# Plain key blocks for near heads, outputs turned by TensorE and a new order in an attention and maxout-FFN kernel

## The chip, the core and the metric

The kernel runs on one core of one Trainium2 chip. The metric is device time in microseconds (us) of one execution; a kernel's time is the median of its runs. Engines are called as in the profile: PE (TensorE matmul), PEld (its weight loads), DVE (VectorE), ACT (ScalarE), POOL (GpSimd) and SP (SyncE, which here only issues DMAs).

## What is computed

Attention over 4 batches, 8 heads, 768 positions, 64 values a head; then a feed-forward layer. Three heads (`is_retrieval` is 1 for heads 0, 2, 6) see all earlier keys. The other five, the near heads, see the 4 first keys (`n_sink`) and the last 64 (`window`).

```python
causal = rel >= 0                      # rel = query - key
stream_keep = causal & (is_sink | in_win)
scores = np.where(mask, scale * q @ k.T, -1e9)
a = softmax(scores); attn = a @ v      # (4, 8, 768, 64)
x = attn.transpose(0, 2, 1, 3).reshape(4 * 768, 512)
h = np.maximum(np.maximum(x @ w1, x @ w2), x @ w3)   # w: 512 x 768
out = h @ w_out                        # 768 x 512, result 3072 x 512
```

## The kernel before

The kernel assumes which heads are near (`GUESS`), computes on that assumption in `fast`, and at the end reads a count of differences; only if it is not zero, `general` computes all anew. Everything of interest is in `fast`. No scheduler decides anything: the tuple `PROGRAM` (line 84) lists 486 steps, and each step emits its instructions at once. So each engine and each DMA queue executes its share strictly in the order of PROGRAM, and a step whose input is late holds up all that follows it on that engine.

Each batch is cut into two halves of 384 queries. Batch 0 goes another way than the others, since it must start from nothing. The steps (table at line 807):

- `hl half hp n`: load K and Q of `n` pairs of heads (line 198), on SP or ACT. For `n` = 2 the staging tiles come from a pool with two buffers each for K and Q, so the third such load waits until the casts of the first have been done.
- `cast half hp xy`: K and Q of a pair to f16 (line 216), K by the first engine named, Q by the second (d DVE, a ACT, p POOL). The tile is position-major, so the copy also exchanges the order of head and position.
- `turnp`: turn K and Q of a pair by TensorE into PSUM, and copy out by the engines named (line 228). `tr` tiles, V's `vb`, the AV results and the feed-forward results share four PSUM banks (`bank`, line 190).
- `s0 half u hp`: scores of batch 0, unit `u` of a pair (line 581). `FIRST_UNITS` lists its key blocks: kind `p` is a plain block of 128 keys, kind `c` a block put together of the sink keys and the 64 keys before a block's middle (`kx0` makes it, line 555). In half 0 the masks are added by TensorE, as a product of the identity with blocks of `far` (0 or -30000; `FIRST_FAR`); then ACT takes Exp into a `pt` tile. Score tiles have two PSUM buffers.
- `k0`: masks of batch 0's half 1, by multiplication (line 634).
- `load_v`: V (line 290). `vc` casts, `vt` sorts V's rows by TensorE (batch 0 alone), `v` casts for other batches, `y` fills `vx`, V's rows for the `c` blocks (line 512).
- `load b quad`: K and Q of batches 1 to 3 for four heads, on POOL's queue (line 248); `turn` transposes a part of them on DVE (line 264, 1.1 us each); `kx` makes their `c` blocks.
- `s`, `k`: scores with Exp and masks of batches 1 to 3 (lines 639 and 696).
- `av b half hp [D]`: probabilities times V, a reciprocal and a product on DVE (line 703); with `D`, a transposing DMA on SP's queue makes `xT`; without it, `x` turns the result by TensorE and a copy (line 736). Seven of the eight results of batch 0's half 1 and batch 1's half 0 go by DMA (from `av 0 1 0 D` to `av 1 0 3 D`), `av 0 1 3` and all of batch 0's half 0 by TensorE.
- `f b half wi ni`: one of 3 x 6 products of a half with a block of w1, w2 or w3 (line 434), with the maximum taken on DVE; `o`: the output product, a copy and the write (line 454).
- `w wi`: load a weight with a cast on POOL's queue. `gs`, `gp`: a tiny copy that holds SP's or POOL's queue until a weight or a load is there. `idle n`: matmuls of zeros. `check`, `verdict`, `read`, `flags`, `guess`: the test of the assumption.

## Time and profile before

| what | value |
|---|---|
| median of 3 runs (lowest, highest) | 195.14 us (192.91, 195.88) |
| the profiled execution | span 195.2 us |
| instructions | 4739 |
| PE busy | 180.9 us, 93% |
| DVE, ACT, POOL busy | 145.0, 98.8, 81.8 us |
| HBM read, written | 25.17 MB, 6.29 MB |

In the profile, a row of a timeline is: start in us, duration in us, engine, line, operation, out<-in, shape, count, and in brackets the idle time before it with what released it. A row of the chain is start, duration, engine, tile and line: the work that ended last, followed back. A row of a group has after the count the busy total in us, the mean of one in ns, and the idle time before it. A row of stretches has the stretch in us, its length, then the busy time and instruction count of PE, PEld, DVE, ACT and POOL, the granted clock of TensorE, the DMA share and GB/s. A row of DMA issues ends with the KB of one and the median us from issue to landing.

### The profile page before, as it was taken

What the parts mean: (1) busy time and instruction counts of PE and PEld (TensorE: products, weight loads), DVE (VectorE), ACT (ScalarE), POOL (GpSimd) and SP (SyncE); (2) the same over time, 40 slices, a digit from 0 to 9 for tenths busy, and PEclk for the clock granted to TensorE, in tenths of its full rate; (3) what the DMA queues carried; (4) which work ended last, traced back from release to release, by engine and by line L of the source; (5) the groups of instructions that cost most, each with busy time, mean ns of one, the idle gap of its engine ahead of it and who ended that gap; (6) DMA issues with size and microseconds to landing.
All of it is one profiled execution on the core that took longest, in us unless ns stands there. A gap on an engine that the chain in (4) does not pass through costs nothing.

```text
span 195.2 us, 4739 instructions
## 1 busy us (share of the span) xinstructions
PE 180.9 (93%) x1854; PEld 106.1 (54%) x1854; DVE 145.0 (74%) x308; ACT 98.8 (51%) x158; POOL 81.8 (42%) x140
## 2 busy tenths in 40 slices
...
GB/s 177 329 325 267 207 213 207 116 164 189 160 187 227 97 133 158 242 99 108 210 167 241 93 58 0 77 114 57 0 66 129 0 57 59 134 0 54 161 54 116
DMA packets 44248, 26.59 MB, mean 136 GB/s; under 512 B 31038, under 2 KB 39742, under 8 KB 44222
## 3 DMA queue, kind: packets, MB, share of 16 engines
...
HBM read 25.17 MB, written 6.29 MB: 161 GB/s over the span
## 4 chain that ended last, share of the span: by engine, by line
PE 66%; DMA 12%; DVE 11%; SPq 5%; issue 2%; ACT 1%; ACTq 0%; DVEq 0%
PE yy L437 34%; PE yy L462 15%; DMA vs<-in_v_dram 8%; PE oacc L717 6%; PE st L674 5%; DMA qs<-in_q_dram 4%; SPq L302 4%; DVE KQ L272 4%; PE yst L437 3%; DVE x L724 2%; DVE acc L449 1%; PE yst L462 1%; DVE KQ L241 1%; SPq L283 1%; DVE vx L800 1%
## 5 line engine op out<-in xcount | busy, mean ns | idle before, releaser
L377 POOL TENSOR_TENSOR pt<-pt,kb 128x512 f16<-128x512 f16 (+5 forms) x53 | 48.3, 931 | 67.4 <-ACT pt L691 55.5
L691 ACT ACTIVATE pt<-st 128x1024 f16<-128x1024 f32 (+2 forms) x51 | 43.5, 908 | 24.6 <-PE st L674 24.2
L437 PE MATMUL yy<-xT,w2t 128*128 128x384 f16 x184 | 36.8, 330 | 0.0
L437 PE MATMUL yy<-xT,w0t 128*128 128x384 f16 x180 | 34.9, 326 | 0.6 <-DMA xT<-x 0.6
L437 PE MATMUL yy<-xT,w1t 128*128 128x384 f16 x176 | 34.4, 326 | 0.1
L462 PE MATMUL yy<-woutt,hT 128*128 128x512 f16 (+1 forms) x138 | 32.8, 384 | 0.0
L449 DVE TENSOR_TENSOR hT<-yy,acc 128x384 f16<-128x384 f32 x46 | 25.2, 555 | 6.8 <-PE yy L437 5.1
L449 DVE TENSOR_TENSOR acc<-yy,acc 128x384 f16<-128x384 f32 x44 | 24.0, 555 | 7.9 <-PE yy L437 4.0
L272 DVE STREAM_TRANSPOSE KQ<-kq 128x384 f32<-128x384 f32 x24 | 25.4, 1134 | 0.4 <-DMA kq<-in_q_dram 0.4
L437 PEld LDWEIGHTS <-w0t 128*128 128x128 f16 x192 | 18.1, 98 | 13.5 <-issue 1.7
L445 ACT CAST acc<-yy 128x384 f16<-128x384 f32 x27 | 12.9, 489 | 23.3 <-PE yy L437 21.2
L437 PEld LDWEIGHTS <-w1t 128*128 128x128 f16 x192 | 17.9, 98 | 12.3 <-issue 1.0
L437 PEld LDWEIGHTS <-w2t 128*128 128x128 f16 x192 | 17.8, 98 | 12.3 <-issue 0.9
L462 PEld LDWEIGHTS <-hT 128*128 128x128 f16 x150 | 14.8, 101 | 16.5 <-issue 2.0
L717 PE MATMUL oacc<-va,pt 128*128 128x65 f16 x392 | 19.1, 195 | 4.4 <-ACT va L478 3.5
L717 PEld LDWEIGHTS <-pt 128*128 128x128 f16 x472 | 17.6, 98 | 8.3 <-issue 4.4
L471 ACT COPY ot<-yy 128x512 f32<-128x512 f32 (+1 forms) x14 | 7.9, 566 | 23.6 <-PE yy L462 20.9
L724 DVE TENSOR_TENSOR x<-oacc,sums 128x384 f16<-128x384 f32 x32 | 17.8, 557 | 1.1
L629 ACT ACTIVATE pt<-st 128x1024 f16<-128x1024 f32 (+5 forms) x22 | 15.5, 760 | 3.1 <-PE st L608 2.9
L674 PE MATMUL st<-KQ 32*128 32x128 f16 (+2 forms) x342 | 15.3, 263 | 0.0
L377 DVE TENSOR_TENSOR pt<-pt,kb 128x256 f16<-128x256 f16 (+4 forms) x31 | 11.7, 383 | 1.8 <-ACT pt L691 1.7
L445 DVE CAST acc<-yy 128x384 f16<-128x384 f32 x18 | 10.0, 557 | 3.8 <-PE yy L437 3.3
...
## 6 DMA issues: line engine op xcount, KB each, us to landing
...
kq<-in_q_dram POOLq DMA_DIRECT2D x3, 288.0 KB, 10.0
...
```

Of the source, the lines that this page charges most:

```text
L272: nc.vector.transpose(out=dst.rearrange("c (p j) -> c j p", j=n)[:, j0:j1], in_=src.rearrange("c (j i) -> c j i", i=R),)
L377: engine.tensor_tensor(out=x, in0=x, in1=of_blocks(kb, pattern, rows), op=ALU.mult)
L437: nc.tensor.matmul(yy[:, 0:HALF], w_t[wi][:, ks, ni * P : (ni + 1) * P], xT[b, half, ks].rearrange("p a t -> p (a t)"), start=(ks == 0), s ...
L445: op(out=acc[b, half, ni], in_=yy[:, 0:HALF])
L449: nc.vector.tensor_tensor(out=acc[b, half, ni] if wi == 1 else hT[b, half, ni], in0=yy[:, 0:HALF], in1=acc[b, half, ni], op=ALU.max,)
L462: nc.tensor.matmul(yo[:, 0:n], hT[b, half, ns][:, tb * P : (tb + 1) * P], woutt[:, ns, c : c + n], start=(ns == 0), stop=(ns == NNB - 1),)
L471: op(out=ot[:, c : c + n], in_=yo[:, 0:n])
L629: nc.scalar.activation(out=pts[0, half, hp, u][:, r0:r1, c0:c1], in_=sts[hp][:, r0:r1, c0:c1], func=AF.Exp, scale=sc,)
L674: nc.tensor.matmul(sts["XY"[g // 2]][:, g % 2, c0 : c0 + n * P], KQ[rows, 0, ki * P : (ki + 1) * P] if kind == "p" else kx[b % 2][quad][ro ...
L691: nc.scalar.activation(out=pts[b, s, xy][:, r0:r1, c0:c1], in_=st[:, r0:r1, c0:c1], func=AF.Exp, scale=sc,)
L717: nc.tensor.matmul(o[:, i, r, 0 : D + 1], at[b, h, kind, ki, qi], vv[:, 0 : D + 1], start=(n == 0), stop=(n == len(todo) - 1), skip_group_ ...
L724: nc.vector.tensor_tensor(out=x, in0=o[:, :, :, 0:D], in1=rc.unsqueeze(3).to_broadcast([P, HB, 2, D]), op=ALU.mult,)
```

## The change

It does five things. In batch 0's half 0 the near heads take plain key blocks (`FIRST_UNITS`, `av`), with the sinks and the window in the mask that TensorE adds; so `far` has six blocks, `kx0` and `y` serve batch 0 only from the third block on, and the retrieval and near heads of a pair get the same columns. Casts of K and Q write through the exchanged view and read the staged tile as it lies. All outputs of batch 0's half 1 and batch 1's half 0 are turned by TensorE. There is no `gs` step any more, `guess` is the last but one step. And PROGRAM is written in a new order throughout; of it the diff below shows the first part and the end.

```diff
@@ -59,7 +59,7 @@
 FIRST_UNITS = [
     {
         "R": [[("p", 0, 0, 3, 0), ("p", 2, 2, 1, 384)], [("p", 1, 1, 2, 0)]],
-        "S": [[("p", 0, 0, 2, 0), ("p", 1, 1, 1, 256), ("c", 1, 2, 1, 384)], [("p", 2, 2, 1, 0)]],
+        "S": [[("p", 0, 0, 3, 0), ("p", 2, 2, 1, 384)], [("p", 1, 1, 2, 0)]],
     },
     {
         "R": [
@@ -74,7 +74,7 @@
         ],
     },
 ]
-FIRST_FAR = {"R": [[(0, "C"), (384, "C")], [(0, "C")]], "S": [[(0, "B0 W B W")], [(0, "B")]]}
+FIRST_FAR = {"R": [[(0, 0, 1), (384, 0, 1)], [(0, 0, 1)]], "S": [[(0, 1, 4)], [(0, 4, 2)]]}
 FIRST_KEEP = {
     ("R", 0): (384, "C"), ("R", 1): (384, "C"), ("R", 3): (0, "C"),
     ("S", 0): (0, "W B W B"), ("S", 1): (0, "W B"),
@@ -82,71 +82,74 @@
 LEAST, MOST = 1.0e-9, 16.0
 
 PROGRAM = (
-    "idle 11, hl 0 2 2 sc, cast 0 1 pd, turnp 0 1 aa, cast 0 0 dd, cast 0 2 dp, load_v 0 0 0 4 s",
-    "load_v 0 0 4 4 s, turnp 0 0 ad, cast 0 3 pa, cleark 0 p, cleark 1 d, kx0 0 1 p, s0 0 1 1",
-    "s0 0 0 0, hl 1 0 2 ss, idle 1, turnp 0 3 da, turnp 0 2 da, s0 0 1 0, kx0 0 3 p, s0 0 0 3",
-    "vc 0 0 4 p, vc 0 4 4 p, s0 0 0 1, kx0 0 2 p, s0 0 0 2, hl 1 2 2 ss, cast 1 0 dd",
-    "turnp 1 0 dd, cast 1 3 dd, load 1 0, vt 0 02 da, cast 1 2 aa, vt 0 1 a, cast 1 1 pp",
-    "turnp 1 1 d, w 0, y 0 0 1:4:2 r p, s0 0 1 2, s0 0 1 3, y 0 0 4:5:1 r r, turnp 1 3 ad",
-    "s0 1 3 0, y 0 0 5:8:2 s r, clear 0 d, kx0 1 1 p, y 0 0 1:4:2 s p, s0 1 1 1, load_v 0 1 s",
-    "turnp 1 2 dd, kx0 1 2 r, av 0 0 1, s0 1 2 0, y 0 0 5:8:2 r r, kx0 1 3 r, w 1, gs 1, s0 1 0 1",
-    "av 0 0 0, av 0 0 3, s0 1 0 2, x 0 0 1 d, x 0 0 0 d, load 1 1, s0 1 3 2, vc 1 0 4 p",
-    "x 0 0 3 a, y 0 0 4:5:1 s p, av 0 0 2, vc 1 4 4 p, s0 1 0 0, s0 1 0 3, vt 1 1 a, turn 1 0 0 0",
-    "clear 1 p, k0 1 1 2 p, x 0 0 2 d, vt 1 02 ad, turn 1 0 1 1, turn 1 0 0 1, s0 1 1 0",
-    "k0 0 0 2 p, k0 0 1 2 d, f 0 0 0 3 a, k0 1 0 2 p, f 0 0 0 1 a, s0 1 1 3, w 2, y 0 1 1:4:2 r p",
-    "s0 1 1 2, y 0 1 4:5:1 r r, gs 0, k0 0 3 2 d, f 0 0 0 5 a, kx 1 0 a, k0 2 1 0 p, turn 1 0 1 0",
-    "k0 3 0 2 p, av 0 1 0 D, av 0 1 1 D, f 0 0 0 4 a, turn 1 1 0 0, turn 1 1 0 1, f 0 0 0 2 a",
-    "f 0 0 0 0 a, f 0 0 1 0, load 2 0, f 0 0 1 5, turn 1 1 1 1, s0 1 2 2, k0 2 0 1 p",
-    "turn 1 1 1 0, f 0 0 1 3, f 0 0 1 2, k0 2 0 0 p, y 0 1 5:8:2 r a, f 0 0 1 1, k0 3 1 2 p",
-    "f 0 0 1 4, s 1 0, av 0 1 2 D, kx 1 1 p, k0 2 1 1 p, k0 2 3 1 p, av 0 1 3, f 0 0 2 0",
-    "f 0 0 2 1, s 1 1, f 0 0 2 5, k 1 0 X 1 d, k 1 1 Y 0 p, f 0 0 2 2, turn 2 0 0 0, f 0 0 2 4",
-    "turn 2 0 1 0, x 0 1 3 a, s 1 2, f 0 0 2 3, f 0 1 0 5 a, f 0 1 0 3 a, k 1 1 X 1 p",
-    "turn 2 0 1 1, f 0 1 0 1 d, s 1 7, k 1 2 X 0 p, f 0 1 0 2 d, flags, load_v 1 0 s, v 1 0 0 d",
-    "y 1 0 1:8:2 s a, v 1 0 1 a, gs 0, k 1 2 Y 0 d, y 1 0 4:5:1 s r, k 1 0 Y 0 p, f 0 1 0 0 d",
-    "w 3, v 1 0 2 d, f 0 1 1 2, s 1 3, f 0 1 2 2, f 0 1 1 1, load_v 1 1 s, k 1 3 Y 0 p, f 0 1 1 3",
-    "f 0 1 2 3, y 1 0 4:5:1 r a, y 1 0 1:8:2 r a, gs 0, f 0 1 0 4 d, s 1 5, k 1 0 X 0 d",
...
-    "f 3 0 1 5, f 3 0 2 0, f 3 1 0 4 a, f 3 1 0 3 a, f 3 1 1 4, read, f 3 0 2 5, f 3 1 0 1 d",
-    "f 3 1 0 5 d, f 3 1 0 0 a, f 3 1 0 2 d, f 3 1 1 2, f 3 1 1 3, f 3 1 1 5, gs 0, o 2 1 0 a",
-    "f 3 1 1 0, f 3 1 2 0, o 3 0 1 d, o 3 0 2 d, o 3 0 0 a, f 3 1 2 2, f 3 1 2 3, f 3 1 1 1",
-    "f 3 1 2 1, f 3 1 2 4, f 3 1 2 5, o 3 1 0 a, o 3 1 1 a, o 3 1 2 d, idle 1",
+    "clear 0 p, cast 0 0 pp, idle 6, hl 0 2 2 sc, turnp 0 0 dd, s0 0 0 0, cast 0 1 pd, idle 1",
+    "load 1 0, turnp 0 1 da, s0 0 0 1, hl 1 0 2 ss, s0 0 1 0, cast 0 3 pp, turnp 0 3 da",
+    "s0 0 0 3, s0 0 1 3, cast 1 0 dp, turnp 1 0 dd, s0 0 1 1, s0 1 0 0, cast 0 2 dd",
+    "cast 1 1 pd, turn 1 0 1 1, turnp 1 1 d, k0 0 0 2 d, idle 1, s0 1 3 0, turn 1 0 0 0",
+    "turnp 0 2 ad, turn 1 0 0 1, cleark 0 d, s0 1 1 0, w 0, load 1 1, idle 1, hl 1 2 2 ss",
+    "cast 1 2 pa, s0 1 2 0, turnp 1 2 aa, kx0 2 d, s0 0 1 2, idle 1, load_v 0 0 4 4 s",
+    "vc 0 4 4 d, cast 1 3 ap, load_v 0 0 0 4 s, s0 0 0 2, s0 1 0 2, vc 0 0 4 d, turnp 1 3 dd",
+    "kx0 3 d, vt 0 02 dd, y 0 0 5:8:2 s d, kx0 1 a, vt 0 1 a, s0 1 0 1, av 0 0 1, s0 1 1 1",
+    "av 0 0 0, s0 1 1 3, k0 2 0 1 p, load_v 0 1 s, vc 1 4 4 a, av 0 0 2, idle 1, k0 0 1 2 p",
+    "vc 1 0 4 p, y 0 0 4:5:1 s p, w 1, x 0 0 0 a, k0 1 0 2 p, clear 1 d, av 0 0 3, vt 1 1 a",
+    "x 0 0 2 d, x 0 0 3 d, s0 1 1 2, k0 0 3 2 d, turn 1 0 1 0, x 0 0 1 a, vt 1 02 aa",
+    "y 0 1 5:8:2 r p, s0 1 3 2, y 0 0 1:4:2 s d, turn 1 1 0 0, s0 1 2 2, f 0 0 0 3 a",
+    "k0 2 3 1 p, turn 1 1 0 1, f 0 0 0 1 a, f 0 0 0 2 a, k0 2 0 0 d, turn 1 1 1 0",
+    "f 0 0 0 0 a, kx 1 0 p, f 0 0 0 4 a, turn 1 1 1 1, s0 1 0 3, k0 3 0 2 d, y 0 1 4:5:1 r r",
+    "gp 1 2, y 0 1 1:4:2 r p, k0 1 1 2 p, f 0 0 0 5 a, av 0 1 1, k0 3 1 2 p, s 1 0, av 0 1 0",
+    "k0 2 1 1 p, av 0 1 3, x 0 1 1 a, k0 2 1 0 p, av 0 1 2, x 0 1 0 a, cleark 1 p, s 1 1",
+    "load_v 1 0 s, y 1 0 1:8:2 s r, w 2, x 0 1 3 d, k 1 1 X 0 d, f 0 0 1 3, f 0 0 1 0",
+    "kx 1 1 p, k 1 0 X 1 p, k 1 0 Y 0 d, f 0 0 1 1, x 0 1 2 a, flags, s 1 2, f 0 1 0 1 d",
+    "f 0 1 1 1, k 1 2 X 1 d, f 0 0 1 5, f 0 0 1 2, s 1 4, f 0 1 2 1, load_v 1 1 s",
+    "f 0 1 0 3 a, y 1 1 4:5:1 r p, k 1 1 Y 0 d, k 1 1 X 1 d, y 1 0 1:8:2 r p, v 1 0 2 a",
+    "f 0 0 2 1, k 1 2 X 0 p, v 1 0 3 d, y 1 0 4:5:1 r r, v 1 0 0 r, y 1 1 1:8:2 r p",
+    "f 0 0 2 2, k 1 2 Y 0 d, s 1 3, f 0 0 1 4, v 1 1 3 p, f 0 0 2 4, load 2 0, f 0 0 2 5",
+    "k 1 0 X 0 d, f 0 0 2 0, k 1 4 X 1 p, f 0 1 1 3, f 0 1 2 3, w 3, av 1 0 0",
+    "y 1 0 4:5:1 s a, s 1 5, k 1 5 X 1 d, f 0 1 0 0 d, av 1 0 3, f 0 1 0 2 a, av 1 0 2",
+    "v 1 0 1 a, f 0 0 2 3, s 1 7, k 1 7 X 0 p, k 1 7 Y 1 p, av 1 0 1, f 0 1 0 4 d, load 2 1",
...
+    "f 2 1 2 2, f 3 0 1 5, f 3 0 2 5, f 2 1 2 1, check, f 3 0 0 4 a, o 2 1 2 d, o 2 1 0 a",
+    "f 3 1 0 3 d, f 3 0 1 4, f 3 1 2 4, verdict, f 3 1 1 3, o 2 1 1 d, f 3 1 0 0 a, f 3 1 2 3",
+    "read, f 3 0 2 4, o 3 0 0 a, o 3 0 2 d, f 3 1 0 2 a, f 3 1 1 2, f 3 1 1 0, f 3 1 2 0",
+    "f 3 1 0 1 a, f 3 1 1 1, f 3 1 2 1, f 3 1 2 2, o 3 0 1 a, f 3 1 2 5, o 3 1 1 d, o 3 1 0 d",
+    "o 3 1 2 a, idle 1, guess, idle 1",
 )

@@ -217,7 +220,7 @@
         cast[half, hp] = []
         for nm, src, op in zip(("kn", "qn"), staged.pop((half, hp)), engines):
             x = half16.tile([P, HB, 2, D], FP16, tag=nm, name=nm)
-            op(out=x, in_=src.rearrange("p h j d -> p j h d"))
+            op(out=x.rearrange("p j h d -> p h j d"), in_=src)
             cast[half, hp].append(x)
 
     def of_pair(hp):
@@ -327,6 +330,10 @@
     nc.vector.memset(warm, 0.0)
     nc.scalar.activation(out=warm, in_=warm, func=AF.Exp)
 
+    far = consts.tile([P, 6, P], FP16, name="far")
+    nc.vector.memset(far[:, 3], -FAR)
+    if n_sink > 0:
+        nc.vector.memset(far[0:n_sink, 3], 0.0)
     kb = consts.tile([P, len(BLOCKS), P], FP16, name="kb")
     nc.gpsimd.memset(kb, 1.0)
     nc.gpsimd.affine_select(
@@ -351,13 +358,18 @@
     )
     for x in (kb[:, 0:1], kb[:, 5:7]):
         nc.vector.tensor_copy(out=x, in_=kb[:, 3:4].to_broadcast([P, x.shape[1], P]))
+
+    def as_far(dst, src):
+        nc.vector.tensor_scalar(
+            out=dst, in0=src, scalar1=FAR, scalar2=-FAR, op0=ALU.mult, op1=ALU.add
+        )
+
+    as_far(far[:, 5], kb[:, 4])
     if n_sink > 0:
         nc.vector.tensor_copy(out=kb[0:n_sink, 0], in_=kb[0:n_sink, 2])
         nc.vector.memset(kb[0:n_sink, 1:5:3], 1.0)
-    far = consts.tile([P, 5, P], FP16, name="far")
-    nc.vector.tensor_scalar(
-        out=far, in0=kb[:, 0:5], scalar1=FAR, scalar2=-FAR, op0=ALU.mult, op1=ALU.add
-    )
+    as_far(far[:, 1:3], kb[:, 0:2])
+    as_far(far[:, 0:5:4], kb[:, 2:4])
 
     def pick(at0, rows, row, a, sa, b, sb):
         inner = [[1, b * P]] if sb == 1 else [[sb * P, b], [1, P]]
@@ -510,22 +522,24 @@
             op(out=va[0][:, :, half * HB + i, 0:D], in_=vb.rearrange("p (h d) -> p h d", d=D))
 
     def prep_x(b, half, heads, what, op):
-        by_row = b == 0 and half in sorted_halves
-        vs = staged_v[b, half] if not by_row else va[0][:, :, half * HB : (half + 1) * HB, 0:D]
+        first = 1 if b == 0 else 0
+        vs = staged_v[b, half] if b else va[0][:, :, :, 0:D]
         dst = vx[b % 2]
         hs = slice(*map(int, heads.split(":")))
         which = list(range(*hs.indices(H)))
         xs_ = slice(near.index(which[0]), near.index(which[-1]) + 1)
         n = len(which)
         assert near[xs_] == which
-        if what == "r":
+        if what == "r" and b == 0:
+            op(out=dst[64:P, xs_, 1:4, 0:D], in_=vs[64:P, hs, 2:5])
+        elif what == "r":
             s0 = 2 * half
             k0 = (1, 0)[half]
             op(out=dst[64:P, xs_, s0 : s0 + 2, 0:D], in_=vs[64:P, hs, k0 : k0 + 2])
         else:
             op(
-                out=dst[0:64, xs_, :, 0:D],
-                in_=vs[0:64, hs, 0:1].to_broadcast([64, n, 4, D]),
+                out=dst[0:64, xs_, first:4, 0:D],
+                in_=vs[0:64, hs, 0:1].to_broadcast([64, n, 4 - first, D]),
             )
 
     at, pts = {}, {}
@@ -542,6 +556,7 @@
                 x = t.rearrange("p n (m c) two -> p (n m) (c two)", m=2)
                 if quad == 0:
                     engine.memset(x[:, 0:4], 0.0)
+                engine.memset(x[:, 4 - 4 * quad : 8 : 4, 64:P], 0.0)
                 x = x[:, 4 - 4 * quad : 8, n_sink:64]
             else:
                 x = t.rearrange("p n c two -> p n (c two)")[:, :, 2 * n_sink : 128]
@@ -552,17 +567,16 @@
             :, 512 * (hp % 2) : 512 * (hp % 2) + 512
         ].rearrange("p (n c) -> p n c", c=P)
 
-    def far_keys_first(half, hp, op):
+    def far_keys_first(hp, op):
         src, dst = of_pair(hp)[:, 0], kx_pair(hp)
-        n0 = 2 * half
         op(
-            out=dst[:, n0 : n0 + 2, 64:P],
-            in_=src.rearrange("p (n c) -> p n c", c=P)[:, n0 + 1 : n0 + 3, 64:P],
-        )
-        if half == 0 and n_sink > 0:
+            out=dst[:, 1:4, 64:P],
+            in_=src.rearrange("p (n c) -> p n c", c=P)[:, 2:5, 64:P],
+        )
+        if n_sink > 0:
             op(
-                out=dst[:, :, 0:n_sink],
-                in_=src[:, 0:n_sink].unsqueeze(1).to_broadcast([P, 4, n_sink]),
+                out=dst[:, 1:4, 0:n_sink],
+                in_=src[:, 0:n_sink].unsqueeze(1).to_broadcast([P, 3, n_sink]),
             )
 
     def far_keys(b, quad, op):
@@ -588,11 +602,10 @@
             pts[0, half, hp, u] = pair_tile()
         if half == 0:
             for hp, r, f in live:
-                for n, (c, x) in enumerate(FIRST_FAR["SR"[f]][u]):
-                    m = len(x.split())
+                for n, (c, at0, m) in enumerate(FIRST_FAR["SR"[f]][u]):
                     nc.tensor.matmul(
                         sts[hp][:, r, c : c + m * P], ident,
-                        of_blocks(far, x),
+                        far[:, at0 : at0 + m].rearrange("p n c -> p (n c)"),
                         start=(n == 0), stop=False, skip_group_check=True,
                     )
         todo = {
@@ -707,7 +720,7 @@
             qi = half * HB + i
             for r in range(2):
                 h = 2 * hp + r
-                if GUESS[h]:
+                if GUESS[h] or (b == 0 and half == 0):
                     use = [("p", ki) for ki in range(qi + 1)]
                 else:
                     use = [("c" if qi > 1 else "p", qi - 1)] * (qi > 0) + [("p", qi)]
@@ -827,7 +840,7 @@
         idle=lambda n: idle_work(int(n)),
         clear=lambda j, e: clear_v(int(j), engines[e]),
         cleark=lambda j, e: clear_k(int(j), engines[e]),
-        kx0=lambda half, hp, e: far_keys_first(int(half), int(hp), ops[e]),
+        kx0=lambda hp, e: far_keys_first(int(hp), ops[e]),
         kx=lambda b, quad, e: far_keys(int(b), int(quad), ops[e]),
         flags=compare_flags,
         check=check_sums,
```

76 rows, old and new, of the table PROGRAM are left out of this document.

## Prediction, made before the changed kernel was run

> **What bounds the kernel now.** I read the page's head first, then busy time by stretches, then the chain that ended last, then the timeline at the two places where TensorE does not run.
>
> ```profile
> span 195.2 us, 4739 instructions
> PE 180.9 (93%) x1854; PEld 106.1 (54%) x1854; DVE 145.0 (74%) x308; ACT 98.8 (51%) x158; POOL 81.8 (42%) x140
> GB/s 177 329 325 267 207 213 207 116 164 189 160 187 227 97 133 158 242 99 108 210 167 241 93 58 0 77 114 57 0 66 129 0 57 59 134 0 54 161 54 116
> ```
> ```profile
> 60.00:65.00 5.00, 1.50 (x29) 1.26 (x30) 2.34 (x7) 2.85 (x4) 0.00 (x0) 0.80 1.07 203
> 65.00:70.00 5.00, 5.00 (x32) 2.29 (x28) 3.39 (x6) 2.04 (x3) 2.87 (x4) 0.52 0.53 76
> ```
> The columns are the stretch, busy time of PE, PEld, DVE, ACT, POOL, granted clock, DMA share, GB/s. TensorE is busy without a break from 65 on, at a granted clock that is 0.52 in the mean up to 70: 0.50 until 69.8, if it is 1.00 from there.
>
> ```profile
> 25.42 0.17 PE tr L740 x3
> ...
> 82.25 1.31 PE oacc L717 x42
> 83.56 0.56 PE st L674 x12
> ...
> 104.12 0.76 PE yy L437 x4
> ...
> 111.39 8.45 PE yy L437 x52
> ...
> 178.80 3.88 PE yy L462 x18
> ...
> 190.56 0.27 ACT ot L471
> ```
> ```profile
> 1.28 4.34 PE L324 MATMUL idl<-zero 128*128 128x512 f16 x11 [1.28 <-DVE warm L327]
> ...
> 26.49 1.47 PE L437 MATMUL yy<-xT,w0t 128*128 128x384 f16 x8
> ...
> 61.28 1.04 ACT L526 CAST vx<-vs 64x1024 f16<-64x1024 f32 x1 [4.45 <-DMA vs<-in_v_dram]
> 63.62 0.50 ACT L478 CAST va<-vs 128x384 f16<-128x384 f32 x1
> 64.17 0.65 PE L717 MATMUL oacc<-va,pt 128*128 128x65 f16 x9 [3.50 <-ACT va L478]
> 71.22 0.59 ACT L471 COPY ot<-yy 128x512 f32<-128x512 f32 x1 [0.74 <-PE yy L462]
> ```
> The chain gives TensorE's steady prices: an `f` (4 matmuls) 8.45/13 = 0.65, an `o` (6) 3.88/3 = 1.29, one AV matmul 1.31/42 = 0.031. A score step `s` takes 0.56, and the `f` behind one (104.12) 0.76 instead of 0.65: 0.67 in all. From the row at 71.22, PROGRAM still holds 119.3 us at these prices; 71.2 + 119.3 = 190.5, which is where the last output copy starts. So from 71 on the kernel is pure TensorE time. From the first `f` at 26.49, 155.5 us remain (144 `f` 93.6, 24 `o` 31.1, 24 `s` 16.1, 429 AV 13.3, the rest 1.4); 26.5 + 155.5 = 182.0, so 8.5 are lost on the way. 3.5 of them are the wait at 64.17: ACT stands in order behind a copy of V that waits for its load, and the next V part is behind it. About 2.8 more are half of the 5.6 us until 69.8 at the halved clock. About 2.2 are small waits. The end is thus: start of the first `f`, plus remaining work, plus what is lost, plus 195.2 − 190.5 = 4.7 of tail.
>
> **The change, part by part.** *Turning by TensorE.* Seven more `x`: 3 transposes each (0.17 by the row at 25.42), 1.2 on the path. They come with a copy each, like those at L241 below: 0.49 on ACT or 0.57 on DVE (4 and 3), counted with those engines. They take seven transposes off SP:
>
> ```profile
> 31.51 9.27 SPq L730 DMA_TRANSPOSE xT<-x  x3
> ```
> Behind these three stood the V loads of batch 1, then the gates, then batch 2's V for which ACT waits at 61.28. In the new order `load_v 1 0` to `2 0` wait for no gate and no transpose on SP, only for free `vs` buffers, and leave by about 33, long before their use near 60. I take the 3.5 + 2.8 as gone. What is late next is DVE, below.
>
> *Plain blocks.* 5 more AV matmuls, 0.15. Scores, masks by TensorE and Exp keep the same columns in unit 0; unit 1 becomes one 2x256 Exp. `kx0` runs 3 times instead of 8, `y` copies 3 places instead of 4. The three `far` steps instead of one cost DVE 0.4 more at about 4, where DVE then waits for K and Q; without that cover it would be 0.4.
>
> *Casts by head.* The same elements, with the turned side now the output. The cast is 0.55 on DVE (L220 below) and the copies at L241, whose output is turned, 0.57; so between 0 and 0.02 each, and I take nothing.
>
> *`guess` at the end.* Its register loads stand behind the last work, beside the last output's landing (the 4.7): nothing. No row shows such a load there; if it does not fit beside the landing, I bound it by 1, an estimate: a quarter of the tail.
>
> *The order.* This is where I see the cost.
>
> ```profile
> 4.08 1.51 SPq L295 DMA_DIRECT2D vs<-in_v_dram  x2
> ...
> 8.46 1.51 SPq L206 DMA_DIRECT2D ks<-in_k_dram  x2
> ...
> 11.41 0.37 SPq L295 DMA_DIRECT2D vs<-in_v_dram  x1
> ```
> ```profile
> vs<-in_v_dram SPq DMA_DIRECT2D x1, 768.0 KB, 9.4
> ```
> ```profile
> L629 ACT ACTIVATE pt<-st 128x1024 f16<-128x1024 f32 x10 | 10.0, 1028 | 1.6 <-PE st L608 1.5
> L241 DVE COPY KQ<-tr 128x384 f16<-128x384 f16 x8 | 4.3, 566 | 0.8 <-PE tr L238 0.7
> L241 ACT COPY KQ<-tr 128x384 f16<-128x384 f16 x6 | 2.6, 488 | 2.5 <-PE tr L238 2.5
> L220 DVE CAST kn<-ks 128x384 f16<-128x384 f32 x4 | 2.2, 550 | 1.8 <-DMA ks<-in_k_dram 1.8
> L272 DVE STREAM_TRANSPOSE KQ<-kq 128x384 f32<-128x384 f32 x24 | 25.4, 1134 | 0.4 <-DMA kq<-in_q_dram 0.4
> L449 DVE TENSOR_TENSOR hT<-yy,acc 128x384 f16<-128x384 f32 x46 | 25.2, 555 | 6.8 <-PE yy L437 5.1
> ```
> Before, batch 0's V is issued at 4.08 and 11.41 and everything of batch 0 is ahead of batch 1. Now the third pair of K loads (`hl 1 2 2`) needs the buffer (2 of them) that `cast 0 2` frees, and on DVE `cast 0 2` stands behind `cast 1 0` and both copies of `turnp 1 0`. Walked by the rows: POOL clears `va` first, casts pair 0 by 6.1 and issues `load 1 0` by 7.7. First scores 7.9, Exp to 9.0, Q of pair 1 copied 9.5, scores, Exp to 11.2, second Exp 11.7, Q of pair 3 copied 12.2, scores and the turn of `1 0` to 13.9, DVE's copies to 14.7, `cast 0 2` 15.3 and 15.8. So `hl 1 2 2` leaves at 15.3 instead of 8.46, and both halves of V behind it, from about 17.4.
>
> By then `load 1 0`, `w 0` and `load 1 1` run on POOL's queue. The V load above needed 9.4 us, from 11.41 to 20.8, though at the 325 GB/s of slices 3 and 4 its 0.79 MB are 2.4 us: with some 3 us of K and Q ahead of it (five loads of 0.2 MB), it had about half of the engines from 13 on. At one half from 16.5, K and Q (2.4 us of work) land at 21.3 and V's first half, in two parts, at 23.7 and 26.1; the second half of V, when POOL's two loads have drained at 28, at 29.5.
>
> Then: DVE's casts to 27.0 (twice the 0.55 of 384 elements, less overlap), sorting by TensorE and DVE's copies (behind the last pair's copies and `kx0 3`) to 30.0, AV 30.0 to 33, the x's and V's second half on an ACT that holds Exps back to back, `xT1` 36.0. The first `f` starts at 36.0 instead of 26.5. What remains then is 156.2: the 155.5, plus 8 x turns instead of one (1.2), less two score steps (0.7) and 0.2 of idle matmuls more. So TensorE begins its solid part 9.5 us later and gets back at most 8.5.
>
> *What is lost after that.* `av 0 1` waits for DVE's last turns of batch 1 and POOL's masks: 0.7 by the walk. Summed over PROGRAM from the first `f`, DVE's work by the rows above exceeds TensorE's by 3.2 us at most (near `s 3 1`; before: 1.4). DVE is 1.4 ahead at the start; I take 1.8 of it. Together 2.5; at least 1, and at most 5.
>
> The sum: 36.0 + 156.2 + 2.5 + 4.7 = 199.4, against the profiled 195.2. The median shown (195.14) is the same to 0.1, so no correction is made.
>
> On the share of the queues, the Trainium skill ("DMA: Bandwidth & Descriptors", "Queues, rings and completion order") says that each DMA engine changes between queues after whole packets. If the larger packets of POOL's loads then took most of the time, the first half of V would land about 1 us later and the sum would be 200.4; the 9.4 us row looks like equal shares.
>
> **The rivals.** *Clock down at the start.* The first idle block is 6 matmuls instead of 11 (4.34 us), and between 15 and 30 TensorE has about 6 us of work in 15. The clock fell at 63.0 (0.98 in that slice, 0.50 in the next), 2.3 us after the work stopped at 60.7, and came back only near 69.8. If it is down when AV begins at 30, the 5.4 us of work up to the first `f` take twice as long, and part of the first `f`s: 2 to 4 later, 201.4 to 203.4. Against it: in the first 60 us before, with TensorE also waiting often, the clock never falls: it was 0.98 still in the slice from 62.
>
> ```profile
> 62.00:63.00 1.00, 0.00 (x0) 0.00 (x0) 0.46 (x1) 1.00 (x3) 0.00 (x0) 0.98 1.08 209
> 63.00:64.00 1.00, 0.00 (x0) 0.00 (x0) 0.00 (x0) 1.00 (x2) 0.00 (x0) 0.50 1.03 196
> ```
> The Trainium skill ("TensorE: Matmul & The Clock Gate", "Why this matters for your kernels") allows gaps of about 3 us; the trace shows the fall after 2.3 us without work, so the rows are the stricter.
>
> *The start is late by less.* If SP's loads get two thirds of the engines, V's first half is there at 23 and the first `f` is bound by ACT: about 20 us of copies and Exps back to back from 8, plus some 5 of waits, 33. Then 33.0 + 156.2 + 1.5 + 4.7 = 195.4: the stall's gain pays for the start, no change.
>
> *Faster.* The loads of POOL's queue give way altogether, V's first half lands at 20 as if nothing ran beside it, and all ACT waits close: the first `f` at 29.5 and 29.5 + 156.2 + 0.5 + 4.7 = 190.9. It decides below a first `f` of 30. For it speaks that the SP queue is truly freed; against it, that V is issued behind a buffer freed at 15.3.
>
> **How the numbers follow.** The forecast as worked out (197 to 202 by its own bounds: first `f` from 34.5 to 37, loss 1 to 5) has 0.40; of that I put 0.23 over the bound. The late clock 0.23, all over it. The smaller delay 0.19, no change. Faster 0.18. So faster 0.18, same 0.36, slower 0.46; 2% (3.9 us) is about what a measurement of this kernel tells from no change. The range for 8 in 10 is 191.5 to 203.0: it cuts the lower half of the faster case and the end of the clock case.
>
> **What would show it.** In the profile after: the third pair of `ks` issues on SP near 15 and not before 12; V's issues after 17 and its casts waiting for DMA near 23 to 26; the first `yy` near 36; no wait of TensorE near 60 and no granted clock of 0.5 after 40; from about 60 to the end nothing but TensorE time, 0.65 an `f`. The prediction is wrong if the first `yy` stands before 32, or if a new wait of several us appears after it.

## The result and the profile after

The changed kernel takes 210.0 us in the median (208.30 to 212.02 in 4 runs), beside 194.02 (191.39 to 195.88) for the kernel before: a ratio of 1.0899, 95% interval 1.0707 to 1.1091. It is slower, and by more than the forecast range (191.5 to 203.0) allows. Some runs of either kernel are disturbed and take some per cent longer, and all ratios here compare undisturbed runs. The profiled run took 208.30 and has a span of 206.6, so 7.2 over the 199.4 that was forecast for the span. In every run the time is 1.7 to 1.9 above the span.

In the kernel after, lines have moved: the `f` matmuls are L449 (before L437), `o` is L474 (L462), the casts are L223 (L220), DVE's and POOL's masks L389 (L377), the turns of K and Q of batches 1 to 3 L275 (L272). The head of its page, and its busy time by stretches (columns as before):

```profile
span 206.6 us, 4779 instructions
PE 184.4 (89%) x1875; PEld 107.5 (52%) x1875; DVE 152.4 (74%) x325; ACT 97.9 (47%) x157; POOL 75.0 (36%) x130
PEclk9999559999999999999999999999999999999998
```
```profile
15.00:20.00 5.00, 2.24 (x21) 0.99 (x21) 5.00 (x11) 2.83 (x4) 0.69 (x2) 1.00 1.09 199
20.00:25.00 5.00, 0.50 (x3) 0.24 (x3) 0.30 (x2) 0.00 (x0) 0.51 (x1) 0.57 1.08 252
25.00:30.00 5.00, 2.91 (x19) 1.47 (x21) 1.28 (x4) 3.08 (x6) 0.51 (x1) 0.50 1.10 334
30.00:35.00 5.00, 4.86 (x74) 2.90 (x70) 4.11 (x12) 4.61 (x8) 2.96 (x6) 0.91 1.02 203
60.00:65.00 5.00, 4.22 (x47) 2.33 (x46) 4.76 (x12) 1.13 (x4) 0.00 (x0) 1.00 1.13 201
```

Between 60 and 65, where TensorE had 1.50 of work before, it has 4.22, and the clock stays at 1.00: the stall is gone. From 20 to 25 no compute engine works for more than 0.51 of 5 us, and the DMA is full (share 1.08). The timeline says what they wait for: SP's issues, the casts behind them on POOL, ACT and DVE, TensorE's two gaps, the first AV product, and the first `f`.

```profile
14.55 1.07 SPq L209 DMA_DIRECT2D ks<-in_k_dram  x2
15.78 0.94 SPq L209 DMA_DIRECT2D qs<-in_q_dram  x2
16.76 6.77 SPq L298 DMA_DIRECT2D vs<-in_v_dram  x3
...
23.71 0.51 POOL L223 CAST kn<-ks 128x384 f16<-128x384 f32 x1 [8.03 <-DMA ks<-in_k_dram]
...
26.52 0.51 ACT L223 CAST qn<-qs 128x384 f16<-128x384 f32 x1 [8.40 <-DMA qs<-in_q_dram]
...
24.28 0.50 PE L241 MATMUL tr<-ident,kn 128*128 128x128 f16 x3 [6.89 <-POOL kn L223]
27.09 0.50 PE L241 MATMUL tr<-ident,qn 128*128 128x128 f16 x3 [2.31 <-ACT qn L223]
...
28.57 0.55 DVE L509 CAST vn<-vs 128x768 f16<-128x768 f32 x1
29.48 0.56 DVE L509 CAST vn<-vs 128x768 f16<-128x768 f32 x1 [0.36 <-DMA vs<-in_v_dram]
...
32.87 0.85 PE L730 MATMUL oacc<-va,pt 128*128 128x65 f16 x12
...
39.03 3.42 PE L449 MATMUL yy<-xT,w0t 128*128 128x384 f16 x20
```

The third pair leaves SP at 14.55 to 15.78 (15.3 was forecast), but lands at 23.7 to 26.5 instead of 21.3, and DVE has cast V's first half at 30.0 instead of 27.0. The first `f` starts at 39.03: 3.0 after the forecast and 12.5 after the kernel before. From the end of V's casts to the first `f` it takes 9.0, as in the forecast (27.0 to 36.0), so all of the 3.0 is in the landing of V.

TensorE ends its last `o` (the chain of waits) at 200.93. With the forecast's 156.2 of work, 200.9 − 39.0 − 156.2 = 5.7 are lost behind the first `f` (2.5 forecast, 8.5 before). The tail is 206.6 − 200.9 = 5.7 (4.7 forecast). So 3.0 + 3.2 + 1.0 = 7.2 are to be explained. TensorE's waits behind the first `f`, all those over 0.15:

```profile
46.76 0.34 PE L753 MATMUL tr<-ident,x 128*128 128x128 f16 x3 [0.40 <-ACT pt L704]
55.01 0.82 PE L449 MATMUL yy<-xT,w2t 128*128 128x384 f16 x4 [0.41 <-DMA w2t<-in_moe_w_dram]
60.92 0.81 PE L449 MATMUL yy<-xT,w2t 128*128 128x384 f16 x4 [0.52 <-DVE hT L461]
61.99 0.81 PE L449 MATMUL yy<-xT,w1t 128*128 128x384 f16 x4 [0.26 <-DVE acc L461]
77.35 0.81 PE L449 MATMUL yy<-xT,w2t 128*128 128x384 f16 x4 [2.04 <-DVE hT L461]
132.92 0.81 PE L449 MATMUL yy<-xT,w2t 128*128 128x384 f16 x4 [0.18 <-DVE acc L457]
```

They sum to 3.8; one of them is 2.04. The other 1.9 are in pieces that this view does not show as waits.

### The profile page after: what moved, and what is told of

Read it like the earlier page. It is cut to its first block, busy times and chain, and to the rows that moved or that the text cites. A ratio compares the mean times of both kernels' runs of the same rounds, so it can differ in the third digit from the quotient of the medians.

```text
span 206.6 us, 4779 instructions
## 1 busy us (share of the span) xinstructions
PE 184.4 (89%) x1875; PEld 107.5 (52%) x1875; DVE 152.4 (74%) x325; ACT 97.9 (47%) x157; POOL 75.0 (36%) x130
## 4 chain that ended last, share of the span: by engine, by line
PE 66%; DVE 10%; DMA 9%; POOL 5%; issue 3%; ACT 3%; SPq 1%; DVEq 0%; POOLq 0%; ACTq 0%
PE yy L449 34%; PE yy L474 12%; PE oacc L730 6%; DMA qs<-in_q_dram 5%; PE st L687 5%; DMA w2t<-in_moe_w_dram 4%; PE yst L449 3%; DVE KQ L275 3%; POOL pt L389 2%; PE st L621 2%; DVE KQ L244 1%; ACT pt L642 1%; PE tr L241 1%; DVE pt L389 1%; PE yst L474 1%
## 5 line engine op out<-in xcount | busy, mean ns | idle before, releaser
L389 POOL TENSOR_TENSOR pt<-pt,kb 128x512 f16<-128x512 f16 (+5 forms) x44 | 39.4, 912 | 45.7 <-ACT pt L704 34.5
L449 PE MATMUL yy<-xT,w2t 128*128 128x384 f16 x180 | 35.3, 326 | 3.1 <-DVE hT L461 2.6
L449 PE MATMUL yy<-xT,w0t 128*128 128x384 f16 x180 | 35.5, 326 | 0.0
L449 PE MATMUL yy<-xT,w1t 128*128 128x384 f16 x180 | 35.0, 326 | 0.3 <-DVE acc L461 0.3
L457 ACT CAST acc<-yy 128x384 f16<-128x384 f32 x30 | 14.2, 490 | 37.8 <-PE yy L449 29.1
L474 PE MATMUL yy<-woutt,hT 128*128 128x512 f16 (+1 forms) x138 | 31.9, 372 | 0.0
L449 PEld LDWEIGHTS <-w2t 128*128 128x128 f16 x192 | 18.3, 98 | 16.0 <-issue 3.4
L275 DVE STREAM_TRANSPOSE KQ<-kq 128x384 f32<-128x384 f32 x24 | 25.1, 1130 | 0.0
L449 PEld LDWEIGHTS <-w1t 128*128 128x128 f16 x192 | 18.0, 98 | 12.6 <-issue 1.1
L449 PEld LDWEIGHTS <-w0t 128*128 128x128 f16 x192 | 17.5, 98 | 11.8 <-issue 0.4
L474 PEld LDWEIGHTS <-hT 128*128 128x128 f16 x150 | 14.1, 98 | 15.8 <-DVE hT L461 1.2
L389 DVE TENSOR_TENSOR pt<-pt,kb 128x256 f16<-128x256 f16 (+5 forms) x40 | 20.5, 522 | 2.2 <-ACT pt L704 1.5
L730 PE MATMUL oacc<-va,pt 128*128 128x65 f16 x402 | 19.8, 193 | 0.1
L642 ACT ACTIVATE pt<-st 128x1024 f16<-128x1024 f32 (+4 forms) x21 | 16.1, 802 | 6.6 <-DMA qs<-in_q_dram 4.0
L483 ACT COPY ot<-yy 128x512 f32<-128x512 f32 (+1 forms) x16 | 9.1, 569 | 20.5 <-PE yy L474 19.9
L687 PEld LDWEIGHTS <-KQ 32*128 32x128 f16 x342 | 9.0, 92 | 5.5 <-issue 3.3
## 6 DMA issues: line engine op xcount, KB each, us to landing
ks<-in_k_dram SPq DMA_DIRECT2D x8, 192.0 KB, 5.2
qs<-in_q_dram ACTq DMA_DIRECT2D x4, 192.0 KB, 4.4
```

Source lines behind the costliest of these rows:

```text
L275: nc.vector.transpose(out=dst.rearrange("c (p j) -> c j p", j=n)[:, j0:j1], in_=src.rearrange("c (j i) -> c j i", i=R),)
L389: engine.tensor_tensor(out=x, in0=x, in1=of_blocks(kb, pattern, rows), op=ALU.mult)
L449: nc.tensor.matmul(yy[:, 0:HALF], w_t[wi][:, ks, ni * P : (ni + 1) * P], xT[b, half, ks].rearrange("p a t -> p (a t)"), start=(ks == 0), s ...
L457: op(out=acc[b, half, ni], in_=yy[:, 0:HALF])
L474: nc.tensor.matmul(yo[:, 0:n], hT[b, half, ns][:, tb * P : (tb + 1) * P], woutt[:, ns, c : c + n], start=(ns == 0), stop=(ns == NNB - 1),)
L483: op(out=ot[:, c : c + n], in_=yo[:, 0:n])
```

## The experiments

**Why the loads land late.** First the trace itself. Engine time and bytes of the two queues in the kernel after, in four stretches: 15 to 18, 18 to 21, 21 to 24 and 24 to 27 (q0 is POOL's queue, q1 SP's; columns are packets, MB, share of 16 engines; a share is a sum of packet times and can exceed 100%; a queue with next to nothing is left out):

```profile
q0 software_dynamic: 348, 0.53, 105.9%
```
```profile
q0 software_dynamic: 272, 0.52, 91.2%
q1 hardware_dynamic: 217, 0.17, 21.3%
```
```profile
q0 software_dynamic: 195, 0.47, 79.6%
q1 hardware_dynamic: 293, 0.21, 25.8%
```
```profile
q1 hardware_dynamic: 1393, 1.03, 106.3%
```

SP issues four K and Q loads from 14.55 on and V from 16.76. Its queue gets nothing until 18, a fifth to a quarter of the engine time until 24, and all of it when POOL's queue is empty. Where both queues have work throughout, packets are served one for one (300 of POOL's and 296 of SP's from 19 to 23; 399 and 397 from 16 to 20 in a1 below), but from 18 to 21 POOL's are 1.9 KB each and SP's 0.8 KB. Two moves test it, one at a time and together.

```diff
 PROGRAM (a1: the third pair early)
-hl 1 0 2 ss, s0 0 1 0, cast 0 3 pp, ... cast 0 2 dd, cast 1 1 pd, ... turnp 0 2 ad, ... hl 1 2 2 ss
+hl 1 0 2 ss, hl 1 2 2 ss, s0 0 1 0, cast 0 2 dd, cast 0 3 pp, ... turnp 0 2 ad, cast 1 1 pd, ...
 PROGRAM (a2: POOL's loads late)
-w 0, load 1 1, idle 1, hl 1 2 2 ss, ... cast 1 3 ap, load_v 0 0 0 4 s
+idle 1, hl 1 2 2 ss, ... cast 1 3 ap, w 0, load 1 1, load_v 0 0 0 4 s
```

*a1, expected:* 

> The kernel after, with one thing moved: the third pair of K and Q (`hl 1 2 2`) is issued right behind the second, because its buffer is freed early (`cast 0 2` and `turnp 0 2` stand some places earlier). POOL's queue keeps its loads where they are. Theory 1 (the start is late because these loads are issued at 14.6 to 15.8 and then stand behind the 3.1 MB that POOL's queue has in flight): issue by 9.5, K and Q cast by 17, V landed near 20, first `yy` of `f` at 31 to 33 instead of 39.0, span 199 to 201 instead of 206.6. Theory 2 (POOL's transfers take the engines whenever both queues have work): K and Q still land after 21, first `yy` 36 or later, span over 203. Theory 3 (the order of the work on ACT, DVE and TensorE sets the start, no transfer does): first `yy` 38 to 39, span 206.

*a2, expected:* 

> The kernel after, with POOL's loads `w 0` and `load 1 1` moved behind `cast 1 3`, so that nothing but `load 1 0` stands on POOL's queue while SP loads the third K/Q pair and V. Issues of that pair stay near 15. Theories 1 and 2: K and Q land by 19 instead of 23.7 and 26.5, V by 23, first `yy` at 33 to 35 instead of 39.0, span 201 to 203 instead of 206.6, if `w 0` itself does not become the last to land. Theory 3 (order of the engines): first `yy` 38 to 39, span 206.

*a3, both moves, expected:* 

> Both moves together: the third K/Q pair issued early, and POOL's `w 0` and `load 1 1` behind `cast 1 3`. Theories 1 and 2: first `yy` at 29 to 32, span 197 to 200, and more than the better of the two moves alone only if the early issue still shares with POOL's queue. Theory 3: first `yy` 38, span 205 to 206. What this cannot mend, by my sum, is the loss after the first `f` (5.7) and the tail (5.7): so 195 is not passed.

(The three loads of POOL that these texts put at 3.1 MB, `load 1 0`, `w 0` and `load 1 1`, are 768 KB each: 2.4 MB. The first of them had moved by 14, so 1.6 MB stood beside SP's loads.) Measured: a1 207.86, ratio 1.0858 (1.0791 to 1.0926); a2 203.33, 1.0613 (1.0529 to 1.0697); a3 202.50, 1.0586 (1.0481 to 1.0691). Spans 206.6, 201.6 and 199.8. V's issues, the casts that wait for DMA and the first `f`, a1 (with TensorE's wait for V) and then a2:

```profile
11.21 3.58 SPq L295 DMA_DIRECT2D vs<-in_v_dram  x3
...
18.78 0.51 POOL L220 CAST qn<-qs 128x384 f16<-128x384 f32 x1 [3.51 <-DMA qs<-in_q_dram]
...
25.40 0.56 DVE L506 CAST vn<-vs 128x768 f16<-128x768 f32 x1 [4.96 <-DMA vs<-in_v_dram]
...
27.41 2.86 PE L514 MATMUL vb<-vn,every 64*128 64x512 f16 x9 [5.69 <-DVE vn L506]
...
37.12 3.42 PE L446 MATMUL yy<-xT,w0t 128*128 128x384 f16 x20
```
```profile
19.88 0.51 POOL L220 CAST qn<-qs 128x384 f16<-128x384 f32 x1 [2.45 <-DMA qs<-in_q_dram]
...
23.34 0.56 DVE L506 CAST vn<-vs 128x768 f16<-128x768 f32 x1 [1.50 <-DMA vs<-in_v_dram]
...
32.86 3.42 PE L446 MATMUL yy<-xT,w0t 128*128 128x384 f16 x20
```

Issuing early mostly moves the wait: K and Q come sooner, but V, issued from 11.21 on, stands beside POOL's loads in their place. DVE's casts of its first half end at 27.35 instead of 30.04, and the first `f` comes 1.9 earlier. Taking POOL's loads out of the way brings the first `f` from 39.03 to 32.86; both moves together give 32.35, just outside the 29 to 32 that was expected. So the place of POOL's loads decides far more than the time of SP's issue, as theory 2 has it. Its sign for K and Q in a1 was wrong all the same: they landed before 19, not after 21. Theory 1 asked for 31 to 33 from a1 and is wrong; theory 3 is wrong for a2.

**The clock and the order of the engines.** In a3 TensorE is busy from 15 to 25 but at a granted clock of 0.50. Twelve more idle matmuls in the places where it waits, here marked:

```diff
-idle 6, hl 0 2 2 sc, ... turnp 0 1 da, s0 0 0 1, ... turnp 0 3 da, s0 0 0 3, ... turn 1 0 1 1
+idle 8, hl 0 2 2 sc, ... idle 1, turnp 0 1 da, idle 1, s0 0 0 1, ... idle 2, turnp 0 3 da, idle 3,
+idle 1, s0 0 0 3, ... idle 2, turn 1 0 1 1
```

*b4, expected:* 

> The kernel with both moves (third K/Q pair early, POOL's loads late), and 12 more idle matmuls laid where TensorE waits for its first casts (2 more in the first block, the others ahead of or behind the turns and scores up to 17). In that kernel the granted clock is 0.50 from 15 to 25 and TensorE is busy there, first `yy` 32.4. Theory (the halved clock at the start is what is left of the delay): the clock stays at 1.0, the 10 us take 5 to 6, first `yy` at 27.5 to 29.5, span 195 to 197 instead of 199.8. Rival (TensorE only waits faster: ACT's Exps and V's landing bound it): first `yy` at 31.5 to 32.5, span 199 to 200. If the idle matmuls come in the way of real work, later than 32.4.

Measured: 201.44, ratio 1.0520 (1.0458 to 1.0582), span 199.7. The same two stretches in a3 and then in b4, and b4's first `f`:

```profile
15.00:20.00 5.00, 4.13 (x27) 1.66 (x25) 4.53 (x7) 3.44 (x6) 3.36 (x7) 0.50 1.10 333
20.00:25.00 5.00, 5.00 (x33) 2.36 (x33) 3.50 (x14) 4.61 (x9) 0.56 (x2) 0.50 1.19 228
```
```profile
15.00:20.00 5.00, 3.72 (x36) 1.78 (x35) 4.07 (x7) 3.99 (x7) 3.61 (x7) 1.00 1.11 333
20.00:25.00 5.00, 4.14 (x36) 1.86 (x36) 4.78 (x17) 5.00 (x11) 0.54 (x2) 1.00 1.18 220
```
```profile
31.20 3.42 PE L447 MATMUL yy<-xT,w0t 128*128 128x384 f16 x20
```

The clock is back at 1.00, and the first `f` comes only 1.15 earlier (32.35 in a3), nearer to the rival's 31.5 to 32.5 than to the theory's 27.5 to 29.5. V landed a little later in b4, though: DVE's casts of its first half end at 23.01 instead of 22.43. From their end to the first `f` it takes 9.9 in a3, 9.0 in the kernel after, and 8.2 in b4 and in its descendants c2 and c3 below. So the halved clock costs 0.8 to 1.7 here, and the landing of V sets the rest. ACT is now full from 20 to 25 (5.00 of 5.00). That behind the DMA and the clock stands the new order itself, which puts more of half 1 and batch 1 ahead of the first `f`, is argued here; c4 below, with the old start, has its first `f` at 27.40.

**The parts without the order.** Each of the three code parts was laid into the order of the kernel before.

```diff
 PROGRAM (b1: TensorE turns alone; the four gates gs 1, gs 0, gs 0, gs 0 ahead of av 1 0 are dropped)
-av 0 1 0 D, av 0 1 1 D, ... av 0 1 2 D, ... av 1 0 0 D, ... av 1 0 3 D
+av 0 1 0, av 0 1 1, ... x 0 1 0 a, x 0 1 1 a, ... av 0 1 2, x 0 1 2 d, ... av 1 0 0, ... x 1 0 0 a,
+x 1 0 1 a, x 1 0 2 d, x 1 0 3 a
 cast_pair (b2: casts by head alone)
-            op(out=x, in_=src.rearrange("p h j d -> p j h d"))
+            op(out=x.rearrange("p j h d -> p h j d"), in_=src)
 PROGRAM (b3: plain blocks alone, with the code of the change for them)
-kx0 0 1 p, kx0 0 3 p, kx0 0 2 p, y 0 0 1:4:2 r p, y 0 0 4:5:1 r r, y 0 0 5:8:2 r r
-kx0 1 1 p, kx0 1 2 r, kx0 1 3 r
+kx0 1 p, kx0 2 r, kx0 3 r
```

*b1, expected:* 

> The kernel before, with one part of the change alone: the seven outputs that SP's DMA turned (`av 0 1 0` to `2`, `av 1 0 0` to `3`) are turned by TensorE (`x` steps, 4 copies on ACT and 3 on DVE), and SP's first four gates, which only held those transposes back, are dropped. Theory (the prediction's): SP is free, V of batches 1 and 2 is issued earlier, the wait of 3.50 at 64 and the halved clock behind it (2.8) go, the seven turns cost 1.2: span 190 to 191 instead of 195.2, ratio 0.975 to 0.985. Rival (the V loads are bound by their buffers or by the engines of the DMA, not by SP): the wait stays, span 195 to 197. Second rival (the DVE and ACT copies fall on the path): the stall goes, but as much is lost in small waits, 194 to 196.

*b2, expected:* 

> The kernel before, with the one line of the casts turned head by head (source read in order, destination strided). The rows of the kernel after say 0.35 us for a DVE cast instead of 0.55, ACT's and POOL's unchanged. Theory: 4 casts of DVE 0.2 shorter each, all ahead of TensorE's first scores, so between 0 and 0.8 us less: span 194.4 to 195.2, ratio 0.99 to 1.0. Rival (TensorE pays for reading the other order): transposes over 0.33 for three, span above 195.5.

*b3, expected:* 

> The kernel before in its order, with the plain blocks alone: near heads of half 0 of batch 0 take plain key blocks, their mask is added by TensorE, `kx0` of half 0 and the `y` copies of their rows are gone, casts as before. Theory: POOL has 3 `kx0` and 2 `y` copies less, ACT's second Exp is one instruction; the first `f` 0 to 1.5 earlier (26.5 before), 0.15 more AV on TensorE: span 194 to 195.5. Rival (the two `far` steps more on DVE delay the first casts): first `f` up to 0.5 later, span 195.5 to 196.

*c1, all three together, expected:* 

> The change without its new order: plain blocks, casts by head and TensorE turns together, laid into the order of the kernel before (its start, its queues, its steps), the first four gates dropped. Theory (the order alone makes the loss, the three code parts are worth about what they measured one by one: +1.1%, -0.6% and about 0): 190 to 194, ratio 0.99 to 1.02, first `yy` at 26 to 28, a loss behind it of 2 to 3. Rival (the parts hurt each other, as by more DVE and ACT copies at the start): first `yy` over 30, ratio over 1.04.

Measured: b1 193.62, ratio 1.0106 (1.0057 to 1.0155); b2 190.56, 0.9942 (0.9884 to 1.0000); b3 192.67, but 195.81 to 199.04 in its three other runs, too far apart for an interval; c1 193.37, 1.0132 (1.0023 to 1.0242). So the three parts together cost about 1%, and the new order makes the rest: 1.09 against 1.013. In c1 the first `f` starts at 26.30. (Of b1's seven copies five are on ACT and two on DVE, not four and three.)

b1 answers the forecast's largest gain. Its 64 us stretch has no stall, as expected, and yet it is slower than the kernel before; its span of 192.0 misses the 190 to 191. The reason is in b2, which has SP's gates and transposes as before and still no stall. The stretch from 60 to 65 of b1 and then of b2 (the row of the kernel before is in the prediction: 1.50 of work, clock 0.80):

```profile
60.00:65.00 5.00, 4.89 (x67) 3.20 (x66) 4.73 (x14) 3.35 (x6) 0.94 (x2) 1.00 0.82 143
60.00:65.00 5.00, 5.00 (x42) 2.54 (x43) 4.12 (x9) 3.11 (x4) 3.24 (x4) 1.00 1.23 159
```

The 3.5 of stall and the 2.8 of halved clock are a matter of the execution. The profiled one had them; that of b2, in the same order of steps, has not. One step was moved to see whether the wait belongs to ACT's place in order, and the casts were timed again:

```diff
 PROGRAM (d1, with the casts of b2; d2 is b2 again)
-load_v 2 0 s, y 2 0 1:8:2 s a, f 0 1 1 5, ... v 2 0 0 a
+load_v 2 0 s, f 0 1 1 5, ... y 2 0 1:8:2 s a, v 2 0 0 a
```

*d1, expected:* 

> The kernel before with the casts by head and one ACT step moved: the copy `y 2 0 1:8:2 s`, behind which ACT stood in order in the execution with the 3.50 wait at 64, comes 30 places later, right before `v 2 0 0`; it costs nothing else. Theory (the wait is not in every execution: it comes when the third load of V of batch 2 lands late, and with it the clock halves; so the 6.3 that the prediction took as a gain are not there in most executions): median as with the casts alone or up to 0.5 lower, 189.5 to 191, ratio 0.985 to 0.995, and no execution above 192.5, while the kernel before beside it shows some at 194 to 197. Rival (the wait moves on to `v 2 0 0` or to the loads behind it): executions of 193 to 197 here too.

*d2, expected:* 

> The kernel before with the casts by head alone, once more and with more rounds: 190 to 191, ratio 0.99 to 0.997 if the four shorter DVE casts gain the 0.2 to 0.8 worked out for them; 1.0 if the first result (0.994, up to 1.0) was chance. Executions of 193 to 197 are expected among them, as in the kernel before, since ACT's copy stands where it stood.

Measured: d2 0.9888 (0.9816 to 0.9959); d1 1.0000 (0.9956 to 1.0044). Of 17 runs of the kernel before beside them, 5 took 195.2 to 196.7; of 6 of d2, 3 took 195.6 to 196.1. Of 12 runs of d1 none lies there, but seven took more than 192.5, one of them 202.23, so its expectation failed. That ACT's place in order makes the long runs is not shown, and d1 loses the 1% of the casts again. In d1's profile TensorE waits 1.76 at 46.86 for a turned output (`xT`) that lands late; b2 and d2 have no such wait. Which part of this is the move and which is the scatter of SP's transposes stays open. The casts alone (b2, d2) are the only version with a ratio below 1, by 0.6 and 1.1%, which is less than the 2% that the prediction gives as what a measurement of this kernel tells from no change.

A part of that gain has its row: DVE's casts of Q, before and in d2.

```profile
L220 DVE CAST qn<-qs 128x384 f16<-128x384 f32 x4 | 2.2, 551 | 2.4 <-DMA qs<-in_q_dram 2.4
```
```profile
L220 DVE CAST qn<-qs 128x384 f16<-128x384 f32 x4 | 1.6, 405 | 2.6 <-DMA qs<-in_q_dram 2.6
```

With DVE's four casts of K (0.550 before, 0.468 in d2) the eight are 0.9 shorter together. That is less than half of the 1.1% (2.1 us) of d2, and d1, with the same casts, gains nothing. The means mix two cases: in b2 and d2 the DVE casts that begin while POOL casts take 0.36 to 0.61, all others 0.35 to 0.36; before, every one takes 0.54 to 0.55.

**The start of before, the rest of after.**

```diff
-(the order of the kernel after up to f 0 0 0 3 a)
+(the order of c1 up to f 0 0 0 3 a), f 0 0 0 3 a, s0 1 1 3, k0 2 0 1 p, k0 1 0 2 p, s0 1 1 2,
+k0 0 3 2 d, turn 1 0 1 0, y 0 1 5:8:2 r p, turn 1 1 0 0, s0 1 2 2
 (the order of the kernel after from there on)
```

*c4, expected:* 

> The start of the kernel before (its order up to the first `f`, with plain blocks, casts by head and TensorE turns), then the order of the kernel after from there on; nine steps of half 1 and batch 1 that only the new start held ahead of the first `f` stand right behind it. Theory (the start is what the new order loses most by): first `yy` at 26 to 28, loss behind it 5 to 8 as in the kernel after, tail 5.5: span 194 to 197, ratio 1.02 to 1.04; so 10 to 12 of the kernel's 206.6 come back. Rival (the late first `f` only held work that must be done anyhow, and it comes back behind the first `f`): loss over 12, span over 200.

Measured: 203.10, ratio 1.0594 (1.0542 to 1.0645), span 202.4, first `f` at 27.40. TensorE's last `o` ends at 196.9. With 156.2 of work and the two score steps that c4 has more behind the first `f` (0.7), 196.9 − 27.4 − 156.9 = 12.6 are lost there: the rival (over 12). The largest piece, and DVE's row ahead of it:

```profile
34.14 2.08 DVE L271 STREAM_TRANSPOSE KQ<-kq 128x384 f32<-128x384 f32 x2 [2.74 <-DMA kq<-in_k_dram]
...
38.50 0.88 PE L683 MATMUL st<-KQ 32*128 32x384 f16 x15 [4.37 <-DVE KQ L271]
```

The scores of batch 1 come early in the new order, and need the turns that the new start had done and the old one had not (DVE waits 2.74 for `load 1 1` and then turns). Another 2.01 is the wait for `hT` of the next part (at 71.47 here), and the clock falls behind both waits (0.79 from 40 to 45, 0.78 from 70 to 75). So the old start cannot be put ahead of the new rest as it is: that rest is laid for the new start. With the new start kept, an earlier first `f` does come back: in a3 it is 6.7 earlier and the span 6.8 shorter.

**What is lost behind the first `f`.** At 73.91 in the kernel after, a DVE mask that takes 0.28 elsewhere (128x256) takes 2.92, while POOL works without a break:

```profile
73.91 2.92 DVE L389 TENSOR_TENSOR pt<-pt,kb 128x256 f16<-128x256 f16 x1
76.75 1.01 DVE L461 TENSOR_TENSOR hT<-yy,acc 128x384 f16<-128x384 f32 x2
```
```profile
73.94 1.19 POOL L389 TENSOR_TENSOR pt<-pt,kb 128x512 f16<-128x512 f16 x1
75.03 0.54 POOL L490 CAST va<-vs 128x384 f16<-128x384 f32 x1
75.49 1.85 POOL L389 TENSOR_TENSOR pt<-pt,kb 128x512 f16<-128x512 f16 x2
```

Behind that mask stands the `hT` for which TensorE waits 2.04. The same mask takes 2.92 in b4 and 2.88 in c4, each time beside the same POOL operations; in the kernel before no DVE mask takes more than 0.83. Two more are long in the kernel after (1.56 instead of 0.68 at 43.94, 2.00 instead of 0.41 at 56.81); what these cost was not followed up. In b4, where all this happens 7.3 earlier, the mask was given to POOL; then two more repairs were added.

```diff
 PROGRAM (c2)
-k 1 5 Y 0 d
+k 1 5 Y 0 p
 PROGRAM (c3, with c2's)
-k0 2 3 1 p, ... w 2, ... idle 1, guess, idle 1
+w 2, k0 2 3 1 p, ... guess, s 2 2, ... idle 1, idle 1
```

*c2, expected:* 

> The kernel with both moves and the idle matmuls (span 199.7), in which DVE's mask `k 1 5 Y 0` takes 2.92 instead of 0.28 while POOL works three operations without a break, and TensorE then waits 2.04 for `hT` behind it. Here that one mask is put on POOL. Theory (the mask stood still because POOL's operations held what both engines need): no DVE mask over 1.0 at that place, the wait of 2.04 gone, span 197.5 to 198. Rival (DVE is simply short of time there): the wait shrinks by 0.3 at most, span 199.4 to 199.7. If POOL's own masks come late instead, a new wait of AV.

*c3, expected:* 

> The last kernel (mask on POOL) with two more repairs: `guess` back in the middle, and `w 2` issued before `k0 2 3 1` on POOL instead of behind its masks. Expected from the rows: the tail 0.9 shorter, the wait of 1.04 for `w2t` gone, so span 195.5 to 196.5, about 1.9 below the last kernel; it stays above the kernel before, since the first `f` stands at 31 instead of 26.4. Rival (the wait for `w2t` only covers another wait): 0.9 less than the last kernel.

Measured: c2 199.89, ratio 1.0404 (1.0308 to 1.0500), span 198.3; c3 196.92, 1.0289 (1.0246 to 1.0332), span 195.1. From the first `f` to TensorE's end c2 takes 193.17 − 32.10 = 161.07, b4 took 194.24 − 31.20 = 163.04: 1.97 less, for a mask of 0.28 moved, and TensorE's wait for that `hT` is gone. (The span misses its 197.5 to 198, since the first `f` came 0.9 later and the wait for `w2t` grew from 1.04 to 1.68.) DVE's row there is now

```profile
67.50 1.17 DVE L459 TENSOR_TENSOR hT<-yy,acc 128x384 f16<-128x384 f32 x2
```

so the collision is confirmed, and a mere lack of DVE time, whose sign was a wait shorter by 0.3 at most, is excluded. In c3 the wait for `w2t` is gone as expected (1.68 in c2), but its first `f` also stands at 29.47, with the same start as b4 (31.20) and c2 (32.10). These 2.6 are V's landing again: its casts end at 21.29 in c3 and at 23.92 in c2. Of c3's 3.2 only 1.4 lie between the first `f` and the last `o`, and its tail is 0.8 longer. With all repairs the new order still stands 2.9% above the kernel before. In spans, the order costs 206.6 − 191.0 (c1) = 15.6; c3 has 11.5 of them back, the scatter of V's landing included. Of the 4.1 that stay, 3.2 are the first `f` (29.47 against 26.30).

**The tail.** `guess` alone, back in its old place:

```diff
-idle 1, guess, idle 1
+... guess, s 2 2, ... idle 1, idle 1
```

*a4, expected:* 

> The kernel after, with `guess` (every engine reads the flags and hints its branch) put back from the end to the middle of the order, before `s 2 2`. If the 1.0 us that the tail grew (5.7 after TensorE's end instead of 4.7) is `guess` standing between the last output and the branch: tail 4.7, span 205.6. If the tail grew because of the last outputs' order: tail stays 5.7, span 206.6, ratio to the kernel before 1.09.

Measured: 208.33, ratio 1.0927 (1.0844 to 1.1010), span 205.9, first `f` at 37.9. The span ends 4.5 after the last DMA issue (201.40) instead of 5.3 (201.31 in the kernel after). Over all profiles, the seven kernels with `guess` at the end take 4.9 to 5.5 from the last issue to the end, and eight of the nine with it in the middle 4.2 to 4.8. That speaks for about 0.8 by `guess`. But the ninth, c3, ends 6.0 after its last issue at 189.12, so this is not settled.

## Why the prediction was wrong

*The start (36.0 forecast, 39.03 measured).* The walk along the instructions was right: `hl 1 2 2` left at 14.55, as soon as the K cast of `cast 0 2` had ended (14.48), and from V's casts to the first `f` it took the 9.0 that was forecast. The step that failed is "at one half from 16.5". The half was read from a V load of 9.4 us, and that row does not show it. In the kernel before, where that load was under way, SP's queue had nearly all of the engines from 14 to 17 and next to nothing from 17 to 21:

```profile
q1 hardware_dynamic: 1146, 0.86, 95.2%
q0 software_dynamic: 34, 0.10, 17.5%
```
```profile
q0 software_dynamic: 336, 0.81, 104.6%
q1 hardware_dynamic: 26, 0.02, 1.7%
```

The load was long because SP's own loads stood ahead of it until 17, and because its last 0.02 MB came beside POOL's loads. There POOL's was the queue that had to wait: its first load was issued at 12.20 and had moved 0.10 MB by 17. In the kernel after SP's share was nothing at first, then 21 to 26%. The rule of the Trainium skill that the prediction weighed ("DMA: Bandwidth & Descriptors", "Queues, rings and completion order", engines change queue after whole packets) agrees with the 300 and 296 packets from 19 to 23. It does not cover the stretch before 18, in which SP's queue got no packet at all. The 1 us that the prediction made of the rule, without a row for the packets' sizes, was too small: V was 3.0 late.

*The clock at the start.* It fell as the rival said (0.57 from 20 to 25, 0.50 from 25 to 30), but the rival wanted it down when AV begins. Its mean from 30 to 35 is 0.91, so it was back at 30.9 if it was 0.50 until then and 1.00 from there, and the first AV product runs at 32.87. By the 9.0 from V's casts to the first `f`, against 8.2 where the clock stayed up (b4, c2, c3), it was worth about 0.8 and not the 2 to 4 that the rival gave. To that extent the forecast's 9.0 was luck: at the full clock this walk is 8.2.

*What is lost afterwards (2.5 forecast, 5.7 measured; at most 5 allowed).* The prediction summed DVE's work against TensorE's and came to 1.8. It had no term for two engines that stop each other. One mask held by POOL's operations makes 2.04 of it, and c2 gives 1.97 back. The Trainium skill has the rule ("SBUF — State Buffer", "SBUF: two separate sides"): a DVE operation with two inputs in SBUF and a GpSimd operation (POOL's) that reads SBUF need the same pair of ports, and the one that starts later waits. The trace agrees in kind, and goes further: here DVE waited through several POOL instructions in a row. About 0.9 more is waits for `w2t` and `hT` as listed; 1.9 are in no listed wait and stay open.

*The stall (gone, as forecast).* It is gone from the kernel after and from b1. But it is gone from b2 too, where SP's gates and transposes stand as before, so the reason that the prediction gave is not shown by this. Its 6.3 were a gain against the profiled execution only. Worked as in the prediction, b2 loses 183.5 − 26.3 − 155.5 = 1.7 behind its first `f`, not 8.5, so there is next to nothing to win back, and b1 loses 1.1%. The forecast's sum took what one execution lost for what the order loses. That execution was among the longest: of 40 executions of the kernel before beside the experiments, 27 have spans of 188.4 to 191.0 and two one above 195.2. The prediction did not see it because it set a span (195.2) against a median of times (195.14), which are 1.7 to 1.9 apart in every run.

*The parts.* TensorE turns, 1.2 on the path: from the first `f` to the last `o` b1 takes 159.4 and b2 157.2, so 2.2 more; 1.2 is the price of the turns, and b1 has a wait of 1.19 for DVE at 36.70. Plain blocks, nothing to speak of: c1 does not contradict it, and b3's runs lie too far apart to say. Casts by head, nothing: wrong by a little; DVE's casts of Q are 0.15 to 0.19 shorter and those of K 0.08, and b2 and d2 stand 0.6 and 1.1% below the kernel before. Two counts are off: of the seven new copies six are on ACT and one on DVE, and `kx0` stood six times in the order before, not eight.

*The tail (4.7 forecast, 5.7 measured).* The bound of 1 that was named for `guess` would cover it, and the kernels with `guess` in the middle speak for it; c3 speaks against it. Open.

*What the sum did not say.* Taken by parts, the order makes 1.09 out of 1.013. c4 shows that one cannot repair it from one end: with the old start it loses 12.6 behind the first `f`. What the 4.1 of c3 are made of, beyond the later first `f`, was not tried.
